# Seven tile pairs of a second dense product as exchanged 64-row halves, key and value weights in one load, and a new order

## The chip, the cores and the metric

The kernel runs on one core of a Trainium2 chip. The core has a matmul engine (PE, whose weight loads the profile shows apart as PEld), a vector engine (DVE), an activation engine (ACT), a general engine (POOL) and a queue engine (SP), which here issues nearly all transfers. The metric is the device time of one execution in microseconds; of the kernel before, three runs gave 151.16, 151.43 and 151.85, with the median 151.43. Lower is better.

## The reference

The sum of three terms over 2048 tokens of 448 values, all in bf16: the input, a linear attention over 16 heads of 28 whose features are softmaxes, and a dense product with Mish between its two weight matrices.

```python
xn = layernorm(x)                                    # x: 2048 x 448
q, k, v = split(xn @ wqkv)                           # 16 heads of 28
phi(y) = concat(softmax(y @ w_phi), softmax(-y @ w_phi))
kv = phi(k)^T v ;  z = sum over tokens of phi(k)
o = (phi(q) kv) / (phi(q) z + 1e-6)
h = xn @ w1 + b1                                     # 2048 x 1792
out = x + o @ wo + (h * tanh(softplus(h))) @ w2      # w2: 1792 x 448
```

## The kernel before

**Tiles.** The tokens are 16 tiles of 128, taken as 8 pairs u (tiles 2u and 2u+1). A row of 448 values is three and a half chunks of 128. The two tiles of a pair share the half chunk: the transposed input of a pair, `xnT[:, u]`, has seven chunks, of which the middle one holds the last 64 values of the one tile in partitions 0 to 63 and those of the other in partitions 64 to 127.

**Half-height passes.** All products over the 448 inputs are made with matmuls that use 64 of the array's 128 rows. Two of them, on different rows, are in the array together and write two different banks of PSUM, one for each tile of the pair. A unit of work on a pair has three parts: A (chunks 0 to 2; rows 0 to 63 work for the first tile and rows 64 to 127 for the second: 6 matmuls), B (the same with the rows exchanged, 6 matmuls) and H (the shared half chunk, 2 matmuls). `passes` lists them. A and H of a bank go on the same rows; B must not run into a bank while A or H does, so `pe_pass` makes each wait for the last part of the other kind on the same banks, and the order puts other work between.

**Steps.** The kernel is a list of named steps, `ORDER`, written out in the file. Each engine runs its instructions in the order in which the steps appear; `Program` derives the waits between engines from what each step reads and writes, and takes PSUM banks from a rotating pool, so the order also sets who waits for whose bank. The steps that matter here (u a pair, t a tile):

- `lx..`, `lkms`, `lvms`, `lkts`, `lps`, `lba`, `l1..`, `l2s`, `los`: loads of x, of the key and the value weights (rows 0 to 383), of the 64 last rows of both (the tails), of the feature weights (Wraw), of b1, of w1, w2 and wo. The last letter is the issuing engine, s for SP and a for ACT.
- `z12`: twelve matmuls on zeros. `b1`: the bias turned by PE. `pv`, `pk`, `pm`, `pw`, `pi`, `pp`, `zero`: constants, on POOL.
- `st`, `rs`, `xn`, `xt`: layer norm of a pair and its transposition. `rs2p` has POOL raise the variance to the power −0.5 (lines 470 and 473); the form with `a` uses a logarithm and an exponential on ACT (lines 476 and 478). `st2b` shares the statistics of a pair between DVE and ACT. `xt2b` and `xt3a` transpose on PE, `xt..m` by a transfer.
- `wtk`, `wmk`, `wmq`: the key and query weights are multiplied by `w_phi` on the chip (lines 556 and 580).
- `vuA`, `kuB`, `quH` and so on: the three products of a pair (line 423); the last part is followed by its evacuation, for k and q two exponentials on ACT.
- `kn`: normalisation of the key features (DVE, then POOL, line 630). `kvu`: the key-value product (line 649, into 32-column groups). `kvz`: its transposition.
- `fq.cA` and so on: first dense product, half q of the tokens, chunk c of 1792 (line 423), with Mish on ACT into `actT`.
- `ndt`: numerator and denominator (line 722, 16 narrow matmuls) and the DVE work on them; `ot`: the transposition of a pair of outputs.
- `woA`, `woB`, `woH`: product with wo (line 845); `gt`: second dense product of tile t (line 828), 14 matmuls over all 128 rows. Both add up in one bank per tile. When all four parts of a tile are in, `finish` adds x on DVE and the bank comes free. Tile 15 is last, and its last 64 columns are made apart (`last_columns`, lines 807 to 810).
- `sto`: stores.

**Queues.** SP, POOL and ACT each run in order. A transfer waits on its issuing engine for what it reads; what stands behind it in that engine's list waits too.

Of the kernel before, what the change touches and what calls it, by code (L numbers as in the profile page):

```python
# [12 lines left out]
D = 448  # L13
H = 16
DH = 28
F = 1792
P = 128
NT = S // P
NU = NT // 2
FC = F // P  # L20
G = 4
# [126 lines left out]
pv table lx2s lba zero pm st2b lx3s lkms lps st3b lkts z12 pi b1 rs2p pw rs3a xn2d bd lx1s wtk0b lvms lx4s xn3d xt2b  # L148
wtk1b wmk0b lqT2 xt3a v2Ha wmk1a v2Ba lqT0 st1 v3Ha lqT1 lqT3 rs1a v3Aa v2Aa st4 rs4p pk v3Ba k3H lx0s k3A qd xn1d
wmq0d wmq1a k2H k3B lx6s pp k2A st5 q3A xn4d k2B q3B rs5p q2A xt1m l1ts q3H k1A q2H xn5p xt4m st0 v1Ad k1H st6 xt5m e7  # L150
rs0p q2B st7 xn0d v1Bd k1B v1Hd rs7p rs6p k4A k4H q1B k4B xn6d q1H q1A v4Ad k5H xn7d v4Hd k5A v4Bd v5Ad kn1.0 xt0m k5B
v5Bd k0B xt6m v5Hd xt7m v0Ba kn2.1 kn2.0 k0H k0A e3 k6H k6A kn0.0 e2 v6Ba l1ms k6B v0Ha kn0.1 v0Aa v6Aa v6Ha k7H k7A
q4B e6 k7B v7Aa v7Ha kn7.0 q4H q4A q6A q6H v7Ba e9 q6B kn6.0 f0.2B kn5.1 f0.0A f1.2A f0.2A f0.0H f1.2H kn6.1 e5 f1.3B
f0.2H f0.0B e12 f1.2B f1.3A kn4.1 f0.3B kn5.0 f1.3H e13 f0.3H f0.1B e4 f0.3A f0.1H f0.1A q7H q0A kn3.1 q0H kn4.0 q5B
e8 q0B q7B kv5 kn7.1 e0 kv0 kv2 q7A q5A f0.13A q5H f0.13B kv7 kv4 e10 kv6 f0.13H f0.6H f0.6A kn3.0 f0.10A f0.6B kn1.1
f0.10B kv3 kv1 ep f0.10H f1.7H f1.7A e11 f1.9A kvz f1.7B f0.12B f1.5B f0.12A f1.5H f0.5H f1.9H f0.12H l2s f1.9B f1.5A
f0.5A f1.1A nd3 f1.1B f0.5B e15 f1.0A f1.1H f1.13B f1.0H f1.13H f1.0B nd2 los f1.13A ot1m f1.8B f0.9H f1.8A f1.8H nd0
f0.11B f0.9A f0.11A f0.11H f0.7A f0.7H f0.8B nd6 e14 f0.8H f0.9B f0.7B e1 f0.8A f1.12H f1.12A f1.10A nd7 f1.10B f1.4H
f1.10H f1.12B ot3m f1.4A nd1 f1.6B f1.4B f0.4H f1.6A ot0m f0.4A wo1H f1.6H f0.4B nd4 wo1A wo3A wo1B wo3H nd5 ot2m g1
g3 g2 f1.11A f1.11H nd11 wo0B f1.11B wo3B wo0A nd13 wo0H nd10 g6 ot5m g0 g7 g11 nd12 wo2A wo5A sto1 ot6m wo5H wo2B  # L160
nd15 nd9 g10 sto0 g5 nd14 ot7m wo2H wo5B nd8 g4 g9 g14 g13 g12 g8 sto3 ot4m wo4H wo4A wo6B wo7B sto2 wo6H wo6A sto5
wo4B sto4 wo7H wob wo7A g15 stt14 sto6 stt15
"""


def run_order(steps, order):
    for name in order:
# [811 lines left out]
```

## Time and profile before

| | us |
|---|---|
| median of three runs | 151.43 (151.16 to 151.85) |
| the profiled execution's own time | 150.73 |
| its span | 148.7 |
| PE busy in the span | 144.0 (97%) |
| DVE busy | 102.7 (69%) |
| ACT busy | 74.7 (50%) |
| POOL busy | 38.9 (26%) |

The profile is one execution, 2.0 us longer than its span. The page gives the busy time of each engine and the chain of work that ended last, followed back from the last instruction. Further views of the same execution give that chain in order of time, the instructions of one engine in a window, and the transfers with their time to landing. Matmuls overlap each other, so the length of one (some 0.35 us) is not what one costs: a stretch is divided by the matmuls in it. Line numbers are those of the kernel before; after the change, lines from 276 on lie 4 lower down.

### The profile page before, as it was taken

The numbers are of one execution on the slowest core, as the hardware profiler recorded it, in microseconds if no ns is written. First come the engines' busy times: TensorE is split into PE (matmuls) and PEld (weight loads), VectorE is DVE, ScalarE is ACT, GpSimd is POOL, SyncE is SP. The second block draws the span as 40 slices with busy tenths as digits, with TensorE's granted clock in tenths as the row PEclk, the third lists the DMA queues.
The fourth block names the chain that finished last, engine by engine and source line by source line (L and its number), as shares of the span: only waits on it lengthen the run. The fifth ranks groups of instructions, "written<-read, shape, count | busy, mean of one in ns | idle before, by whom it ended". The sixth has DMA issues, their size and how long they took to land.

```text
span 148.7 us, 3864 instructions
## 1 busy us (share of the span) xinstructions
PE 144.0 (97%) x1669; PEld 74.2 (50%) x1669; DVE 102.7 (69%) x229; ACT 74.7 (50%) x91; POOL 38.9 (26%) x53
## 2 busy tenths in 40 slices
PE   6899999999999999999999999999999999999992
PEld 2365555555444555444444445545555555555561
DVE  0699898996999930407787989529983999930072
ACT  4997999779999999567747661002000000000000
POOL 4424465179999992000000000000000000000000
PEclk9999999999999999999999999999999999999999
DMA  4997997799699069499956053210013130551005
GB/s 131 245 278 216 119 185 149 126 170 344 103 188 196 14 52 132 85 239 295 195 98 125 4 62 62 43 23 0 7 37 86 35 93 0 123 127 58 4 10 175
DMA packets 39964, 17.23 MB, mean 116 GB/s; under 512 B 33932, under 2 KB 39180, under 8 KB 39948
## 3 DMA queue, kind: packets, MB, share of 16 engines
q1 hardware_dynamic: 39776, 16.89, 54.4%
q8 instruction: 13, 0.21, 0.6%
q10 hardware_dynamic: 172, 0.10, 0.2%
q14 instruction: 3, 0.02, 0.0%
HBM read 7.02 MB, written 1.84 MB: 60 GB/s over the span
## 4 chain that ended last, share of the span: by engine, by line
PE 92%; DMA 3%; DVE 2%; SPq 1%; issue 0%
PE PS L423 50%; PE PS L828 29%; PE PS L845 7%; DMA Wkv<-in_A_wqkv_dram 3%; PE PS L722 3%; PE PS L649 2%; PE PS L580 1%; DVE xn L497 1%; SPq L270 1%; PE PS L556 0%; PE PS L505 0%; DVE x_all L793 0%; DVE Eq L512 0%; DVE x_all L814 0%
## 5 line engine op out<-in xcount | busy, mean ns | idle before, releaser
L423 PE MATMUL PS<-xnT,W 64*128 64x512 bf16 x392 | 44.8, 377 | 0.0
L828 PE MATMUL PS<-W,actT 128*128 128x448 bf16 (+1 forms) x224 | 42.9, 351 | 0.0
L699 ACT ACTIVATE actT<-PS,b1T 128x1024 bf16<-128x1024 f32 x28 | 29.8, 1112 | 22.1 <-PE PS L423 22.1
L828 PEld LDWEIGHTS PS<-W,actT 128*128 128x128 bf16 x224 | 21.5, 98 | 19.8 <-issue 0.3
L423 PEld LDWEIGHTS PS<-xnT,W 64*128 64x128 bf16 x392 | 17.9, 94 | 21.9 <-PE PS L423 1.9
L630 POOL TENSOR_TENSOR actT<-actT,rSk 128x896 bf16<-128x896 bf16 x16 | 26.6, 1699 | 5.1 <-DVE rSk L628 5.1
L793 DVE TENSOR_TENSOR x_all<-PS,x_all 128x448 bf16<-128x448 f32 (+1 forms) x16 | 9.2, 613 | 15.2 <-PE PS L845 10.5
L626 DVE TENSOR_REDUCE Sk<-actT 128x32 f32<-128x896 bf16 x16 | 16.6, 1037 | 1.1 <-ACT actT L618 1.1
L618 ACT ACTIVATE actT<-PS 128x896 bf16<-128x896 f32 x16 | 13.7, 920 | 1.8 <-PE PS L423 1.7
L423 PE MATMUL PS<-Wpk,xnT 64*128 64x448 bf16 x112 | 13.2, 349 | 0.0
L423 PE MATMUL PS<-Wkv,xnT 64*128 64x448 bf16 x112 | 12.9, 349 | 0.0
L423 PE MATMUL PS<-Wpq,xnT 64*128 64x448 bf16 x112 | 12.6, 349 | 0.0
L738 DVE COPY Sq<-PS 128x16 f32<-128x16 f32 x32 | 4.0, 167 | 12.0 <-PE PS L722 12.0
L462 DVE BATCH_NORM_STATS2 stats<-x_all 128x6 f32<-128x448 bf16 x14 | 8.4, 601 | 3.4 <-DMA x_all<-in_A_x_dram 3.4
L746 DVE TENSOR_TENSOR v_all<-v_all 128x464 f32<-128x464 f32 x16 | 10.3, 641 | 0.6
L742 DVE TENSOR_TENSOR v_all<-PS,Sq 128x464 f32<-128x464 f32 x16 | 10.3, 641 | 0.5
L749 DVE TENSOR_TENSOR xn<-v_all,rden 128x448 bf16<-128x448 f32 x16 | 10.0, 625 | 0.6
L744 DVE TENSOR_TENSOR v_all<-PS,Sq 128x464 f32<-128x464 f32 x16 | 10.1, 629 | 0.0
L680 ACT ACTIVATE actT<-PS 128x896 bf16<-128x896 f32 x10 | 8.6, 930 | 0.1
L423 PEld LDWEIGHTS PS<-Wpq,xnT 64*128 64x128 bf16 x112 | 5.4, 94 | 5.0 <-ACT actT L680 0.2
L423 PEld LDWEIGHTS PS<-Wkv,xnT 64*128 64x128 bf16 x112 | 5.4, 94 | 5.1 <-ACT actT L618 0.2
L423 PEld LDWEIGHTS PS<-Wpk,xnT 64*128 64x128 bf16 x112 | 5.3, 94 | 5.1 <-issue 0.2
(83 smaller groups left out, 118.8 us busy)
## 6 DMA issues: line engine op xcount, KB each, us to landing
W<-in_B_w_dram SPq DMA_DIRECT2D x1, 1568.0 KB, 7.9
out_dram<-x_all SPq DMA_DIRECT2D x7, 224.0 KB, 2.2
W<-in_B_w_dram SPq DMA_DIRECT2D x1, 1344.0 KB, 7.0
x_all<-in_A_x_dram SPq DMA_DIRECT2D x4, 224.0 KB, 3.1
x_all<-in_A_x_dram SPq DMA_DIRECT2D x2, 448.0 KB, 4.9
Wkv<-in_A_wqkv_dram SPq DMA_DIRECT2D x2, 336.0 KB, 4.8
Wo<-in_A_wo_dram SPq DMA_DIRECT2D x2, 336.0 KB, 6.3
W<-in_B_w_dram SPq DMA_DIRECT2D x2, 224.0 KB, 4.1
```

What stands on the lines that cost most here:

```text
L423: ins = e.matmul(o, lhs(c, k), rhs(c, k), start=first and n == at[par][0], stop=last and n == at[par][-1])
L618: op("ACT", lambda e, s=s: e.activation(E_of(u)[:, s, :, :], two(b, D), ACT.Exp, scale=1.0 if s == 0 else -1.0), r=[pb(b), pb(b + 1)], w=[ ...
L626: op("DVE", lambda e: e.tensor_reduce(Sk[u][:, s, :], Eh(), AX.X, ALU.add), r=[("E", u, s)], w=[("Sk", u, s)], tag=f"Sk{u}.{s}")
L630: op("POOL", lambda e: e.tensor_tensor(Eh(), Eh(), ap_on(rSk[u][:, s, 0:1], [[1, 2 * H], [0, DH]]), ALU.mult), r=[("E", u, s), ("rSk", u, ...
L699: op("ACT", lambda e: e.activation(actT[:, fc, q * 1024:(q + 1) * 1024], bank(b, 2), ACT.Mish, bias=b1T[:, fc:fc + 1]), r=[("b1T",), pb(b) ...
L742: op("DVE", lambda e: e.tensor_tensor(tv(t1[i]), num(0), sx(1), ALU.mult), r=[pb(b), pb(b + 1), ("Sq", i, 1)], w=[("t1", i)], tag=f"ta{t}")
L744: op("DVE", lambda e: e.tensor_tensor(tv(t2), num(1), sx(0), ALU.mult), r=[pb(b), pb(b + 1), ("Sq", i, 0)], w=[("t2",)], tag=f"tb{t}")
L746: op("DVE", lambda e: e.tensor_tensor(t1[i], t1[i], t2, ALU.add), r=[("t1", i), ("t2",)], w=[("t1", i)], tag=f"tc{t}")
L749: op("DVE", lambda e: e.tensor_tensor(o_sb[(t // 2) % 2][:, t % 2, :].rearrange("p (h d) -> p h d", d=DH), t1[i][:, :, 0:DH], ap_on(rden[i ...
L793: op("DVE", lambda e: e.tensor_tensor(x_all[:, t, 0:n], bank(b)[:, 0:n], x_all[:, t, 0:n], ALU.add), r=[pb(b), ("x", t)], w=[("out", t)], ...
L828: ins = e.matmul(bank(b)[:, 0:width(t)], actT[:, fc, tok(t)], W2[:, fc, 0:width(t)], start=first and fc == 0, stop=last and fc == FC - 1)
L845: ins = e.matmul(bank(b)[:, 0:w], oT_of(u)[lo:hi, cc * P:(cc + 1) * P], Wo[lo:hi, cc, 0:w], start=first and n == at[par][0], stop=last and ...
```

## The change

It has four parts.

1. **Second dense product.** For pairs 0 to 6 the two steps `g2u` and `g2u+1` give way to `GuA` and `GuB`: 28 half-height matmuls each, over the 14 chunks, rows 0 to 63 for the one tile and rows 64 to 127 for the other, and exchanged in B. The helper `out_pair` is shared with the wo parts. A tile of these pairs then has five parts (two of G, three of wo), and both tiles of a pair come to an end with the same part. Pair 7 keeps g14 and g15.
2. **Weights.** One load brings key and value weights (384 rows, of both matrices) where two loads brought 336 KB each.
3. **First pair's norm power** on ACT (`rs2a`; the first pair worked on is pair 2) where it was on POOL; the statistics of the second, pair 3, are all on DVE (`st3`), where they were shared with ACT. b1's load is issued behind the first statistics on ACT.
4. **A new order** of all steps. At the start value products stand ahead of the feature products; at the end the G parts lie between nd steps and wo parts; the q, k, v and f parts between them are in another order as well.

PE at the start, before (L364 the matmuls on zeros, L693 the bias, L556 the transposes of the key weights, L505 those of xn, L580 the feature products, L423 the products of a pair):

```order
L364 MATMUL PS<-zeros 128x512 x12
L693 MATMUL PS<-ident,b_rows 128x14
L556 MATMUL PS<-ident,Wkv 112x128 x8
L505 MATMUL PS<-ident,xn 128x128 x7
L556 MATMUL PS<-ident,Wkv 112x128 x8
L580 MATMUL PS<-Wbd,Eq 128x112 x8
L505 MATMUL PS<-ident,xn 128x128 x7
L423 MATMUL PS<-Wkv,xnT 128x448 x2
L580 MATMUL PS<-Wbd,Eq 128x112 x8
L423 MATMUL PS<-Wkv,xnT 128x448 x26
L423 MATMUL PS<-Wpk,xnT 128x448 x8
```

and in the change, where the same lines have 4 added:

```order
L368 MATMUL PS<-zeros 128x512 x12
L697 MATMUL PS<-ident,b_rows 128x14
L509 MATMUL PS<-ident,xn 128x128 x7
L560 MATMUL PS<-ident,Wkv 112x128 x8
L509 MATMUL PS<-ident,xn 128x128 x7
L560 MATMUL PS<-ident,Wkv 112x128 x8
L427 MATMUL PS<-Wkv,xnT 128x448 x14
L584 MATMUL PS<-Wbd,Eq 128x112 x16
L427 MATMUL PS<-Wkv,xnT 128x448 x14
L427 MATMUL PS<-Wpk,xnT 128x448 x6
```

The transposes of xn now stand ahead of those of the key weights, the two L584 groups are together, and fourteen value matmuls stand ahead of them.

PE towards the end, before (L828 the second dense product, L845 the wo parts, L722 the nd matmuls):

```order
L722 MATMUL PS<-KVZ,EqT 128x60 x16
L828 MATMUL PS<-W,actT 128x448 x56
L722 MATMUL PS<-KVZ,EqT 128x60 x16
L845 MATMUL PS<-Wo,Wkv 128x448 x6
L845 MATMUL PS<-Wo,WqT 128x448 x8
L845 MATMUL PS<-Wo,Wkv 128x448 x6
L722 MATMUL PS<-KVZ,EqT 128x60 x32
L828 MATMUL PS<-W,actT 128x448 x28
L722 MATMUL PS<-KVZ,EqT 128x60 x16
L845 MATMUL PS<-Wo,Wkv 128x448 x2
L845 MATMUL PS<-Wo,WqT 128x448 x6
L722 MATMUL PS<-KVZ,EqT 128x60 x16
```

and in the change, where L848 holds both the wo parts (those from Wo) and the half-height parts of the second product (those from W, actT):

```order
L848 MATMUL PS<-Wo,Wkv 128x448 x2
L848 MATMUL PS<-W,actT 128x448 x28
L726 MATMUL PS<-KVZ,EqT 128x60 x16
L848 MATMUL PS<-Wo,Wkv 128x448 x8
L848 MATMUL PS<-W,actT 128x448 x28
L726 MATMUL PS<-KVZ,EqT 128x60 x16
L848 MATMUL PS<-Wo,Wkv 128x448 x12
L848 MATMUL PS<-W,actT 128x448 x28
L726 MATMUL PS<-KVZ,EqT 128x60 x16
L848 MATMUL PS<-W,actT 128x448 x28
L726 MATMUL PS<-KVZ,EqT 128x60 x16
L848 MATMUL PS<-Wo,Wkv 128x448 x6
```

Long runs of the full-height form are gone from here; what stands in their place are runs of 28 half-height matmuls between nd and wo parts.

SP at the start, before (L270 x, L273 the main weights, L278 their tails, L282 the transposed query weights, L293 the feature weights):

```order
L270 DMA x_all<-in_A_x_dram 128x896 x2
L273 DMA Wkv<-in_A_wqkv_dram 128x3x448
L293 DMA Wraw<-in_A_w_phi_dram 112x4x28
L278 DMA Wkv<-in_A_wqkv_dram 64x896 x2
L270 DMA x_all<-in_A_x_dram 128x896
L273 DMA Wkv<-in_A_wqkv_dram 128x3x448
L270 DMA x_all<-in_A_x_dram 128x1792
L282 DMA_TRANSPOSE WqT<-in_A_wqkv_dram 128x448 x4
L270 DMA x_all<-in_A_x_dram 128x896
L270 DMA x_all<-in_A_x_dram 128x1792
```

and in the change (L277 is the joint load):

```order
L270 DMA x_all<-in_A_x_dram 128x896 x2
L277 DMA Wkv<-in_A_wqkv_dram 128x3x896
L297 DMA Wraw<-in_A_w_phi_dram 112x4x28
L282 DMA Wkv<-in_A_wqkv_dram 64x896 x2
L270 DMA x_all<-in_A_x_dram 128x896
L270 DMA x_all<-in_A_x_dram 128x1792
L286 DMA_TRANSPOSE WqT<-in_A_wqkv_dram 128x448 x4
L282 DMA W<-in_B_w_dram 64x1792 x2
L521 DMA_TRANSPOSE xnT<-xn 128x7x128
L270 DMA x_all<-in_A_x_dram 128x896
L270 DMA x_all<-in_A_x_dram 128x1792
```

The second weight load is gone, the first is twice as wide, and the tails of w1 have moved ahead of the last two loads of x.

The diff, with the table of steps cut to its first line:

```diff
-pv table lx2s lba zero pm st2b lx3s lkms lps st3b lkts z12 pi b1 rs2p pw rs3a xn2d bd lx1s wtk0b lvms lx4s xn3d xt2b
+table lx2s st2b lba zero pi lx3s lkvs lps pv lkts z12 rs2a st3 pk xn2d rs3a xn3d lx1s b1 xt2b wtk0b lx4s xt3a st1
...
+    def load_kv(eng):
+        dma(eng, lambda e: e.dma_start(Wkv[:, 0:3, :], A_wqkv[0:384, D:3 * D].rearrange("(c p) f -> p c f", p=P)),
+            w=[("Wk", 0), ("Wv", 0)], tag="ldKV")
...
     def parts_of(t):
-        return 3 if f"wo{t // 2}F" in STEPS else 4
+        return (2 if f"wo{t // 2}F" in STEPS else 3) + (2 if f"G{t // 2}A" in STEPS else 1)
...
-    def wo(u, part):
+    def out_pair(u, part, todo, works, r, tag):
         places = [out_part(2 * u + par) for par in range(2)]
-        todo = passes(part)
 
         def f(e):
             at = {par: [n for n, x in enumerate(todo) if x[1] == par] for par in range(2)}
-            for n, (c, par, (lo, hi)) in enumerate(todo):
+            for n, (c, par, k) in enumerate(todo):
                 b, first, last = places[par]
-                cc = xchunk(c, par)
                 w = width(2 * u + par)
-                ins = e.matmul(bank(b)[:, 0:w], oT_of(u)[lo:hi, cc * P:(cc + 1) * P], Wo[lo:hi, cc, 0:w],
-                               start=first and n == at[par][0], stop=last and n == at[par][-1])
+                lhs, rhs = works(c, par, k, w)
+                ins = e.matmul(bank(b)[:, 0:w], lhs, rhs, start=first and n == at[par][0], stop=last and n == at[par][-1])
             return ins
-        pe_pass(f, [("oT", u)] + [("Wo", n) for n in range(4)], places[0][0], part, f"wo{u}{part}")
+        pe_pass(f, r, places[0][0], part, tag)
         for par, (b, first, last) in enumerate(places):
             if last:
                 finish(2 * u + par)
+
+    def wo(u, part):
+        def works(c, par, k, w):
+            cc = xchunk(c, par)
+            return oT_of(u)[k[0]:k[1], cc * P:(cc + 1) * P], Wo[k[0]:k[1], cc, 0:w]
+        out_pair(u, part, passes(part), works, [("oT", u)] + [("Wo", n) for n in range(4)], f"wo{u}{part}")
+
+    def ffn2_pair(u, part):
+        x = int(part == "B")
+
+        def works(fc, par, k, w):
+            return actT[k[0]:k[1], fc, tok(2 * u + par)], W2[k[0]:k[1], fc, 0:w]
+        out_pair(u, part, [(fc, r ^ x, HALF[r]) for fc in range(FC) for r in range(2)], works,
+                 [("W2",)] + [("act", fc, u // 4) for fc in range(FC)], f"G{u}{part}")
```

More of the change, by code (lines that the diff above doesn't have):

```diff
@@ L158 @@
[L158 to L162, printed above, removed]
+table lx2s st2b lba zero pi lx3s lkvs lps pv lkts z12 rs2a st3 pk xn2d rs3a xn3d lx1s b1 xt2b wtk0b lx4s xt3a st1
@@ L884, in _kernel @@
             add(f"wo{u}{part}", wo, u, part)
+        for part in "AB":
+            add(f"G{u}{part}", ffn2_pair, u, part)
         for s in range(2):
@@ L911, in _kernel @@
             add(f"l{n}m{c}", load_main, eng, "W" + n, t, A_wqkv[:, (i + 1) * D:(i + 2) * D])
+        add(f"lkv{c}", load_kv, eng)
         add(f"lkt{c}", load_tail, eng, "Wkv", Wkv, A_wqkv[:, D:3 * D])
```

23 lines of the change are left out of this document (14 added, 9 removed).

## The prediction

> **What bounds the kernel now.** I read the page's totals first, then the chain that ended last, in order of time, then the first twelve microseconds engine by engine, then the transfers.
>
> The page, its totals and the shares of its chain:
>
> ```profile
> span 148.7 us, 3864 instructions
> PE 144.0 (97%) x1669; PEld 74.2 (50%) x1669; DVE 102.7 (69%) x229; ACT 74.7 (50%) x91; POOL 38.9 (26%) x53
> PE 92%; DMA 3%; DVE 2%; SPq 1%; issue 0%
> ```
>
> PE carries 92% of the chain, and nothing beside the first load and the last store holds it up. So the change is worth what it does to PE's own stream, plus what it does to the moment when the dense stream begins. The chain in order of time (start, length, what):
>
> ```profile
> 1.72 4.95 DMA Wkv<-in_A_wqkv_dram
> ...
> 9.92 0.50 PE PS L580 x8
> 10.42 3.32 PE PS L423 x34
> ...
> 50.89 0.88 PE PS L649 x96
> ...
> 58.55 0.64 PE PS L649 x64
> ...
> 67.30 3.93 PE PS L423 x36
> ...
> 88.60 1.89 PE PS L845 x20
> 90.49 0.22 PE PS L722 x16
> 90.71 8.05 PE PS L828 x42
> 98.76 0.97 PE PS L423 x8
> ...
> 113.64 0.33 PE PS L722 x16
> ...
> 116.30 5.40 PE PS L828 x28
> 121.70 0.33 PE PS L722 x16
> ...
> 123.01 16.00 PE PS L828 x84
> ```
>
> **Term 1: the matmuls of the second product.** L828 is the full-height form (128 rows, 448 columns). The three pieces give two unknowns: (16.00 − 5.40) / 56 = 0.189 us for one matmul, and 5.40 − 28 × 0.1893 = 0.10 us left over at the start of a run (8.05 − 42 × 0.1893 = 0.10 as well). L845 is the 64-row form of the same width: 1.89 / 20 = 0.0945 each, 0.189 for a pair that does one full-height matmul's work. The 392 new half-height matmuls (7 pairs of tiles × 2 parts × 28) therefore cost the same as the 196 they replace: zero, within 0.1 us. The 64-row weights that each needs load beside the running matmuls, as they do under L845.
>
> **Term 2: switches between the two forms.** A run of L828 pays 0.10 at its start. At its end the next piece pays: 16 matmuls of L722 take 0.22 after half-height work (90.49) but 0.33 after L828 (113.64, 121.70), so 0.11; the eight L423 at 98.76 take 0.97, where 8 × 3.93 / 36 = 0.87. One switch is 0.10. Before has four runs of L828 inside half-height work (g1 g3 g2; g6 g0 g7 g11; g10 g5; g4 to g8), 8 switches, and one into g15. After has one switch, into g14 g15. Eight fewer: −0.8 us. The key-value product L649 is also a different form: (0.88 − 0.64) / 32 = 0.0075 each, 0.64 − 64 × 0.0075 = 0.16 to enter; leaving it I put at the 0.10 above. Three runs of it become two: −0.25. Together −1.05 us. Switches at the start stay five and five, by the order.
>
> On these the Trainium skill, "TensorEngine Tiling (Array Packing)", section "Key Properties", says that changing the tiling mode drains the array. It gives no time; the rows' 0.10 is used.
>
> **Term 3: the start.** What stands on the engines (PE, ACT, POOL, DVE, SP) up to 9 us:
>
> ```profile
> 1.39 4.80 PE L364 MATMUL PS<-zeros 128*128 128x512 bf16 x12 [1.39 <-POOL mask L327]
> 6.72 0.65 PE L556 MATMUL PS<-ident,Wkv 128*112 128x128 bf16 x8 [0.43 <-DMA Wkv<-in_A_wqkv_dram]
> 7.38 0.56 PE L505 MATMUL PS<-ident,xn 128*128 128x128 bf16 x7
> 7.85 0.65 PE L556 MATMUL PS<-ident,Wkv 128*112 128x128 bf16 x8
> 4.37 0.67 ACT L458 ACTIVATE junk<-x_all,rmean 128x448 bf16<-128x448 bf16 x1
> 6.75 0.29 ACT L476 ACTIVATE lnv<-mv,eps_col 128x2 f32<-128x2 f32 x1
> 7.07 0.20 ACT L478 ACTIVATE rstd<-lnv 128x2 f32<-128x2 f32 x1
> 0.80 0.53 POOL L339 MEMSET v_all<- 128x256 uint32 x1 [0.29 <-POOLq L964]
> 5.52 0.71 POOL L473 TENSOR_TENSOR rstd<-lnv,mhalf 128x2 f32<-128x2 f32 x1
> 4.19 0.59 DVE L462 BATCH_NORM_STATS2 stats<-x_all 128x6 f32<-128x448 bf16 x1
> 4.82 0.18 DVE L464 BATCH_NORM_AGGREGATE mv<-stats 128x2 f32<-128x6 f32 x1
> 6.42 0.90 DVE L497 TENSOR_SCALAR xn<-x_all,mv,rstd 128x448 bf16<-128x448 bf16 x3
> 0.84 0.63 ACTq L297 DMA_DIRECT2D b_rows<-in_B_b_dram  x1
> ```
>
> Transfers: KB each, us to landing.
>
> ```profile
> W<-in_B_w_dram SPq DMA_DIRECT2D x1, 1344.0 KB, 7.0
> x_all<-in_A_x_dram SPq DMA_DIRECT2D x4, 224.0 KB, 3.1
> x_all<-in_A_x_dram SPq DMA_DIRECT2D x2, 448.0 KB, 4.9
> Wkv<-in_A_wqkv_dram SPq DMA_DIRECT2D x2, 336.0 KB, 4.8
> W<-in_B_w_dram SPq DMA_DIRECT2D x2, 224.0 KB, 4.1
> Wkv<-in_A_wqkv_dram SPq DMA_DIRECT2D x2, 112.0 KB, 4.6
> ```
>
> Norm power on ACT: the squares end at 5.04; logarithm and exponent take 0.29 + 0.20 and two gaps of some 0.05, so 5.6, where POOL's power ended at 6.23. DVE meanwhile takes the second pair's other statistics (0.59 + 0.18 from 4.9), free at 5.7. Its three scalings (0.90) end at 6.65 and the first transposes of xn can start at 6.7, not 7.38. The bias load, issued on ACT behind the squares (4.4 to 5.0 by its 0.63), feeds a small transpose that stands ahead on PE. No landing is listed for it; I bound it by an issue's end plus 1.0 (the first x load, of 224 KB, lands 3.1 after its issue began) and by 4.1, the 224 KB row under traffic, and take the first: 3.5 KB. The end near 4.1 would put it at 8.5 and cost 1.7.
>
> The joint load is 672 KB where the keys alone were 336, and PE needs the keys. Below: the 112 and 336 KB rows differ by 0.2 in 224 KB, +0.3 for 336 KB more. Above: the x rows, 1.8 us in 224 KB, +2.7. Between: the W1 rows, 2.9 us over 1120 KB, +0.87. The number of source rows stays 384, only their width doubles, and it is ahead of the same small loads; I take +0.6, nearest to the W1 slope. By the Trainium skill, "DMA: Bandwidth & Descriptors", section "Anatomy of one DMA", bytes move at 436 GB/s, an estimate of 0.79; the sum would then be −0.75.
>
> So the keys land at 6.67 + 0.6 = 7.27, and the tails behind them, which released 7.85, at 8.45. PE: xn transposes 6.7 to 7.2, keys' 7.3 to 7.9, second xn transposes to 8.4, keys' second half 8.45 to 9.05. Before's dense stream ran from 10.36 (the L423 behind the L580 of 9.92) with one H part (0.19) and two L580 groups (0.50 with a switch, so 0.40 each) already done. After owes these, and three switches: 9.05 + 0.19 + 0.80 + 0.30 = 10.34. Term 3 is zero, from −0.3 to +2.1 by the ends of the load's price. What hides the value half of the load: its own first use is later still (the H part behind 9.05). Behind the keys on SP wait the small Wraw load, the tails and x; the separate value load is no longer issued there, so the WqT transposes move up by one issue, and x's first pair with them; the W1 tails now stand ahead of the last two x loads, whose statistics stand well behind on DVE.
>
> **Term 4: ACT.** The tightest place that I find is between the last exponentials and Mish (ACT):
>
> ```profile
> 50.85 1.73 ACT L680 ACTIVATE Eq<-PS 128x896 bf16<-128x896 f32 x2
> 52.48 3.35 ACT L680 ACTIVATE actT<-PS 128x896 bf16<-128x896 f32 x4
> 55.84 1.28 ACT L699 ACT_TABLE_LOAD   x1
> 57.14 2.12 ACT L699 ACTIVATE actT<-PS,b1T 128x1024 bf16<-128x1024 f32 x2
> ```
>
> After: from q5's last part to f1.0's first, ACT does six exponentials (4.98), a table load (1.3) and three Mish (3.1): 9.4. PE has q and f parts and eight kv steps between: two q parts of 6 and one of 2 (14 × 0.0945), eight f parts of 6 and four of 2 (56 × 0.109), 7.4 together, and 256 × 0.0075 + 2 × 0.26 = 2.4 for kv: 9.9. It holds, by half a us. Elsewhere the chain of before shows no wait for an evacuation, and I take the new order to keep its distances about as well; I add +0.1 for such waits, from 0 to +1. The tail is the same: g15, eighteen narrow matmuls, two additions, two stores.
>
> **Sum.** −1.05 + 0 + 0.1 = −0.95 against the profiled execution's own 150.73 (span 148.7 and 2.0 around it), which lies 0.7 under the median 151.43. On the median: 150.5.
>
> **Rivals.**
> - *The joint load holds the start.* If it lands 1.6 us later than the keys did instead of 0.6, the gain is gone; at the x rows' +2.7 the time is 151.43 − 0.95 + 2.1 = 152.6. For it: PE's first wait is this load (0.43 at 6.72), and all later loads queue behind it. Against: 112 and 336 KB land alike. Chance 0.13.
> - *The gain is lost in waits, no change: 151.4.* The two parts of a pair may not follow each other: the second waits for the end of the first, since other rows then write the bank. Between G0A and G0B stand only 16 narrow matmuls and one H part (0.22 + 0.22), and 64-row banks are held longer, as half of an output is done early. With ACT's margin this could cost 1 us. Against: L845 and L423 do the same now and the chain shows no wait of theirs. Chance 0.18.
> - *The clock comes later.* The twelve warm-up matmuls took 0.40 us each for 512 columns, when 448 take 0.189 later: half rate up to some 5.5 us. After starts them some 0.4 earlier (the zeros are POOL's first and no longer stand behind its memset of 0.53) and leaves PE idle for longer, from about 5.8 to 6.7. If full rate came only at 9, the 2.1 us of transposes would double: 150.5 + 2.1 = 152.6. The Trainium skill, "TensorE: Matmul & The Clock Gate", section "What's actually happening", has the clock rise after a busy window of about 3.4 us that is free-running, so the moment may fall badly; the one trace cannot show it. Chance 0.07.
> - *A better start*: keys at +0.3 and the bias at once, everything 0.3 earlier: 150.2 and, with no wait on ACT, 150.1; below 149.6 only if a switch is dearer than 0.10. Chance of that 0.02.
>
> **How the numbers follow.** The forecast (149.6 to 150.9) has 0.60, the rivals 0.18, 0.13, 0.07 and 0.02. A measurement of this kernel tells about 0.5% (0.75 us) from no change, so faster begins under 150.7. The forecast's upper edge lies over that: of its 0.60, 0.52 is faster. Faster 0.52 + 0.02 = 0.54; same 0.08 + 0.18 = 0.26; slower 0.13 + 0.07 = 0.20. The range 149.6 to 152.2 takes in the forecast, the case of no change and the nearer half of both slow rivals.
>
> **What would show it.** The chain after: one L828-like run of 28 at the end; pairs of the second product at 0.189; 16 narrow matmuls at 0.22 throughout. Keys' transposes near 7.3 and their second half near 8.45; POOL's first power gone. Wrong if PE waits for the joint load beyond 8, if a wait of PE on Mish or on its own earlier part appears, or if the pairs take over 0.195.

## The result and the profile after

The changed kernel takes 154.86 us (median of six, 153.75 to 155.37) where the kernel before takes 151.36 beside it (150.80 to 151.85): 1.0227 times as long, interval 1.0201 to 1.0253. It was forecast 150.5 us, 0.6% faster; it is 3.5 us slower. The profiled execution took 154.04, 2.0 more than its span, and before's 150.73, so the two traces differ by 3.3. Medians here and below are of all executions of a kernel; where the granted clock parts them into groups, the groups are given.

The page of the changed kernel, its totals, its granted clock (a digit for each fortieth of the span, in tenths of the full clock, 9 for 90% or more) and the shares of its chain:

```profile
span 152.0 us, 4252 instructions
PE 144.7 (95%) x1865; PEld 77.9 (51%) x1865; DVE 102.8 (68%) x231; ACT 73.9 (49%) x88; POOL 37.9 (25%) x51
PEclk9987999999999999999999999999999999999999
PE 91%; DMA 5%; ACT 1%; DVE 0%; issue 0%
```

PE's work is 0.7 us longer (144.7 against 144.0), the span 3.3. So most of the loss is time in which PE had nothing to do. The chain in order of time (start, length, what) says where:

```profile
4.64 5.38 DMA b_rows<-in_B_b_dram
10.02 0.05 issue
10.07 0.19 PE PS L697
10.26 0.86 PE PS L509 x7
11.12 0.85 PE PS L560 x8
11.97 0.75 PE PS L509 x7
12.72 0.79 PE PS L560 x8
13.50 1.43 PE PS L427 x14
...
57.12 1.72 PE PS L653 x160
...
62.88 1.01 PE PS L653 x96
...
89.36 2.65 PE PS L848 x28
92.00 0.22 PE PS L726 x16
...
143.94 5.07 PE PS L832 x28
149.00 0.02 issue
```

The bias load, 3.5 KB issued on ACT behind the squares, is 5.38 us on the way, and PE's first real work (L697, the transposition of the bias) stands behind it. Only then come the transposes of xn and of the key weights (L509, L560). They end at 13.50. By the prediction's account of what was still owed there (one H part, two groups of feature products, three switches: 1.29 us), this is the point 14.79 of a stream that before reached at 10.36: 4.43 us late. From there to PE's last matmul it is 134.2 us (149.00 − 14.79), where before it was 135.0 (145.40 − 10.36). The two rows of before for this, the first from the list of PE's instructions, the second from the chain:

```profile
10.36 2.63 PE L423 MATMUL PS<-Wkv,xnT 64*128 64x448 bf16 x26
142.98 2.42 PE PS L828 x14
```

The new stream is 0.8 us shorter, and another 0.3 is saved behind the last matmul. The start costs 4.4, four times what these two save.

Two things make the start late. One is the wait: the zeros end at 6.25 (3.19 after the start of the first window below), and the transposition of the bias begins at 10.07. The other is the clock. The windows of 3.41 us around it (busy time and, in brackets, instructions of each engine; then granted clock, share of the DMA engines, GB/s):

```profile
core 0: us, PE busy (x) PEld busy (x) DVE busy (x) ACT busy (x) POOL busy (x), PEclk, DMA share, GB/s
3.06:6.47 3.41, 3.19 (x8) 0.88 (x6) 2.67 (x8) 2.54 (x9) 0.63 (x2) 1.00 0.89 247
6.47:9.89 3.42, 0.00 (x0) 0.00 (x0) 1.21 (x5) 0.09 (x1) 0.64 (x2) 1.00 1.08 256
9.89:13.30 3.41, 3.23 (x31) 3.21 (x31) 1.86 (x6) 1.63 (x3) 0.43 (x1) 0.50 1.38 198
13.30:16.71 3.41, 3.41 (x43) 1.97 (x43) 2.99 (x9) 2.48 (x6) 0.00 (x0) 1.00 0.36 95
```

PE has nothing to do from 6.47 to 9.89, and for exactly the next 3.41 us the clock is granted at half. In that stretch fall the transposes: in the list of PE's instructions their groups take 0.93 to 1.06 us, where groups of the same kinds took 0.56 and 0.65 before. Half the clock for 3.41 us takes 1.1% off the mean of a span, so the mean clock of an execution tells how many such stretches it had: 1.0 none, 0.989 one, 0.978 two. Two of the six executions of the changed kernel had one (153.75, 154.04) and four had two (154.85 to 155.37). The kernel before had none: its mean clock was 0.997 or more in all executions beside the experiments. No trace holds a second stretch, so where it lies is not shown.

The joint load, issued at 1.73, landed 7.1 us later, at about 8.8:

```profile
Wkv<-in_A_wqkv_dram SPq DMA_DIRECT2D x1, 672.0 KB, 7.1
```

Here that is hidden behind the bias. Between 18.7 us and PE's last matmul nothing stands in the chain's rows but PE, so no wait on ACT, on Mish or between the two parts of a pair became visible.

### The profile page after: what moved, and what is told of

It is laid out like the page before. It is cut to its first block, busy times and chain, and to the rows that moved or that the text cites. A ratio compares the mean times of both kernels' runs of the same rounds, so it can differ in the third digit from the quotient of the medians.

```text
span 152.0 us, 4252 instructions
## 1 busy us (share of the span) xinstructions
PE 144.7 (95%) x1865; PEld 77.9 (51%) x1865; DVE 102.8 (68%) x231; ACT 73.9 (49%) x88; POOL 37.9 (25%) x51
## 4 chain that ended last, share of the span: by engine, by line
PE 91%; DMA 5%; ACT 1%; DVE 0%; issue 0%
PE PS L427 49%; PE PS L848 31%; DMA b_rows<-in_B_b_dram 4%; PE PS L832 3%; PE PS L726 2%; DMA x_all<-in_A_x_dram 2%; PE PS L653 2%; PE PS L584 1%; PE PS L560 1%; PE PS L509 1%; ACT junk L457 0%; DVE x_all L797 0%; ACT rmean L460 0%; DVE x_all L818 0%; PE PS L697 0%
## 5 line engine op out<-in xcount | busy, mean ns | idle before, releaser
L848 PE MATMUL PS<-W,actT 64*128 64x448 bf16 x392 | 39.4, 349 | 0.0
L848 PEld LDWEIGHTS PS<-W,actT 64*128 64x128 bf16 x392 | 21.1, 94 | 15.2
L466 DVE BATCH_NORM_STATS2 stats<-x_all 128x6 f32<-128x448 bf16 x15 | 9.1, 607 | 3.7 <-DMA x_all<-in_A_x_dram 3.7
```

The lines of the kernel that those rows point to most:

```text
L466: op("DVE", lambda e, t=t: e.bn_stats(stats[:, t, :], x_all[:, t, :]), r=[("x", t)], w=[("st", t)], tag=f"bn{t}")
L848: ins = e.matmul(bank(b)[:, 0:w], lhs, rhs, start=first and n == at[par][0], stop=last and n == at[par][-1])
```

## The experiments

The theory formed from this trace: the whole loss lies in two loads at the start, the bias load's place on ACT and the joint load, together with the clock that falls when PE waits for them; all else of the change does about what was forecast. The rivals: the new order loses time somewhere that the chain does not show; or the halves cost more than full-height matmuls. Medians of the kernel before beside these runs lay between 151.19 and 151.36; differences to it below use 151.2.

### The bias load back ahead of the statistics

```diff
-table lx2s st2b lba zero pi lx3s lkvs lps pv lkts z12 rs2a st3 pk xn2d rs3a xn3d lx1s b1 xt2b wtk0b lx4s xt3a st1
+table lx2s lba st2b zero pi lx3s lkvs lps pv lkts z12 rs2a st3 pk xn2d rs3a xn3d lx1s b1 xt2b wtk0b lx4s xt3a st1
```

> The changed kernel with only the load of the bias moved back ahead of ACT's first statistics, where the kernel before has it. Theory B (the late bias load holds PE from 6.3 to 10.1 and lets the clock fall, and is the whole loss at the start): PE starts near 7.3, time 150.3 to 150.7. Theory B+J (behind it the joint load, which landed at 8.87, is the next bound): the key transposes wait for it to 8.9, dense stream some 1.5 us later than before's, less 0.8 from PE's stream: 151.6 to 152.4, up to 1.1 more if the clock still falls. Theory J alone (the joint load is the cause, the bias is not): no change, 154.5 to 155.

Measured: 152.34 (ten executions, 149.85 to 153.19), 2.5 less than the changed kernel. Eight of the ten had one stretch of half clock (152.21 to 153.19); the two without one took 149.85 and 151.09. PE at the start, and the two windows of the clock:

```profile
6.05 0.18 PE L697 MATMUL PS<-ident,b_rows 14*128 14x14 bf16 x1
6.75 0.56 PE L509 MATMUL PS<-ident,xn 128*128 128x128 bf16 x7 [0.52 <-DVE xn L501]
8.80 0.71 PE L560 MATMUL PS<-ident,Wkv 128*112 128x128 bf16 x8 [1.49 <-DMA Wkv<-in_A_wqkv_dram]
```

```profile
5.86:9.27 3.41, 1.40 (x17) 0.95 (x17) 2.04 (x8) 0.97 (x3) 0.00 (x0) 1.00 1.11 262
9.27:12.68 3.41, 3.41 (x29) 2.38 (x28) 2.36 (x7) 2.55 (x5) 1.08 (x2) 0.50 1.43 245
```

xn is ready at 6.75, as the prediction had it (6.7). But now the joint load comes to light: PE waits 1.49 for the key weights, until 8.80 and not 7.27. And after a window in which PE was busy for 1.40 of its 3.41 us the clock fell.

### The same bias load late, in the kernel before

```diff
-pv table lx2s lba zero pm st2b lx3s lkms lps st3b lkts z12 pi b1 rs2p pw rs3a xn2d bd lx1s wtk0b lvms lx4s xn3d xt2b
+pv table lx2s zero pm st2b lba lx3s lkms lps st3b lkts z12 pi b1 rs2p pw rs3a xn2d bd lx1s wtk0b lvms lx4s xn3d xt2b
```

> The kernel before with only the load of the bias moved behind ACT's first squares. Theory B: the bias lands near 9 to 10, PE waits for it, and the time rises by 3 to 4 us to 154.4 to 155.4, with a fall of the clock. Theory J alone: the bias is not the cause, below 152.

Measured: 154.47 (153.67 to 155.10), 1.0212 of before (1.0165 to 1.0260). One name moved by three places in the table costs the kernel before nearly as much as the whole change cost. PE's wait for it:

```profile
9.21 0.16 PE L693 MATMUL PS<-ident,b_rows 14*128 14x14 bf16 x1 [2.52 <-DMA b_rows<-in_B_b_dram]
```

and the load's own time under way, from the chain:

```profile
4.42 4.66 DMA b_rows<-in_B_b_dram
```

### Early bias and two loads of the weights

```diff
-table lx2s st2b lba zero pi lx3s lkvs lps pv lkts z12 rs2a st3 pk xn2d rs3a xn3d lx1s b1 xt2b wtk0b lx4s xt3a st1
+table lx2s lba st2b zero pi lx3s lkms lps pv lkts z12 rs2a st3 pk xn2d rs3a xn3d lx1s b1 xt2b wtk0b lvms lx4s xt3a st1
```

> The changed kernel with the early bias load and with key and value weights again in two loads, the values behind x's first pair. If the prediction's terms for PE's stream hold (0.8 us gained) and the start is like before's or 0.3 better: 150.2 to 150.8. If the joint load did not matter: the same as with the early bias alone.

Measured: 150.25 (150.18 to 151.25), 0.9935 of before (0.9914 to 0.9955). With both loads put back the rest of the change gives 0.95 us, as much as the prediction's sum; how much of that is luck stands under "The sum" below. No execution had a stretch of half clock. PE at the start:

```profile
6.18 0.19 PE L697 MATMUL PS<-ident,b_rows 14*128 14x14 bf16 x1
6.72 0.58 PE L509 MATMUL PS<-ident,xn 128*128 128x128 bf16 x7 [0.35 <-DVE xn L501]
7.19 0.65 PE L560 MATMUL PS<-ident,Wkv 128*112 128x128 bf16 x8
8.30 0.62 PE L560 MATMUL PS<-ident,Wkv 128*112 128x128 bf16 x8
9.64 1.50 PE L427 MATMUL PS<-Wkv,xnT 64*128 64x448 bf16 x14 [0.72 <-DMA Wkv<-in_A_wqkv_dram]
```

The transposes run almost without a gap from 6.72; what PE waits for now is the value half of the weights, 0.72 us until 9.64, since the new order puts value products first.

### The joint load alone, in the kernel before

```diff
-pv table lx2s lba zero pm st2b lx3s lkms lps st3b lkts z12 pi b1 rs2p pw rs3a xn2d bd lx1s wtk0b lvms lx4s xn3d xt2b
+pv table lx2s lba zero pm st2b lx3s lkvs lps st3b lkts z12 pi b1 rs2p pw rs3a xn2d bd lx1s wtk0b lx4s xn3d xt2b
```

> The kernel before with only the two weight loads made one. Theory B+J: keys land near 8.9 where they landed at 6.7, PE's first real work is 1.5 to 2.2 us later, 152.9 to 153.6. If the joint load does not matter (its landing at 8.87 would then be due to the later order of other loads): 151.2 to 151.9.

Measured: 153.63 (153.63 to 154.12), 1.0168 of before (1.0145 to 1.0191): +2.4. Every execution had one stretch of half clock. The key weights come at 8.33, where they came at 6.72; busy for 1.71 us of a window, PE loses the clock in the next:

```profile
8.33 0.65 PE L560 MATMUL PS<-ident,Wkv 128*112 128x128 bf16 x8 [1.55 <-DMA Wkv<-in_A_wqkv_dram]
```

```profile
6.51:9.93 3.42, 1.71 (x24) 1.36 (x24) 1.88 (x6) 1.61 (x6) 1.47 (x3) 1.00 1.35 265
9.93:13.34 3.41, 3.41 (x32) 2.54 (x32) 3.34 (x11) 2.22 (x5) 0.06 (x1) 0.50 1.04 203
```

So each of the two loads costs over 2 us by itself, in either kernel, the stretch of half clock that it brings included.

### Two loads, the bias load late

Early or late bias, one load or two: this run is the fourth corner of that square.

```diff
-table lx2s st2b lba zero pi lx3s lkvs lps pv lkts z12 rs2a st3 pk xn2d rs3a xn3d lx1s b1 xt2b wtk0b lx4s xt3a st1
+table lx2s st2b lba zero pi lx3s lkms lps pv lkts z12 rs2a st3 pk xn2d rs3a xn3d lx1s b1 xt2b wtk0b lvms lx4s xt3a st1
```

> The changed kernel with two weight loads in place of the joint one, and the bias load left behind the first statistics on ACT. It completes a square: late bias with joint load 154.86, early bias with joint load 152.34, early bias with two loads 150.25. Theory (PE stands first for the bias load, and the loads in front of it set its landing; the joint load alone would hold the keys' transposes, which come later): the bias lands near 9.2 as in the kernel before with its bias load moved, PE begins 3 us later than in the best version, 0.45 of it is taken back where that one waits at v1A, and the clock falls for one window (1.2): 153.5 to 154.3. Rival (the joint load is the larger cost and the bias only lands late because of it): 151.0 to 152.0.

Measured: 152.91 (twelve executions, 150.98 to 154.69). Neither expectation's range holds it: the wait and the fall of the clock are where the theory has them, its price was 0.6 to 1.4 too high. The bias landed earlier than taken, at 8.57, with 336 KB less in front of it than in the changed kernel. The executions order themselves by the mean clock: one at 1.0 took 150.98; seven at 0.989 took 152.19 to 153.23; four at 0.978 took 153.89 to 154.69. By the medians of these groups a stretch of half clock costs some 1.7 us here. The chain of the profiled one (0.989):

```profile
4.51 4.01 DMA b_rows<-in_B_b_dram
...
8.57 0.19 PE PS L697
```

The square, medians in us:

| | two loads | joint load | difference |
|---|---|---|---|
| bias early | 150.25 | 152.34 | +2.1 |
| bias late | 152.91 | 154.86 | +2.0 |
| difference | +2.7 | +2.5 | |

The two add up within 0.2 us: each costs about as much beside the other as alone. But these medians mix executions with and without the half clock. Where the clock held, the early bias with the joint load took 149.85 and 151.09, and the late bias with two loads 150.98, at most 0.8 over 150.25. So in these three executions, which are few, most of the price of one load alone is the fall of the clock behind its wait, and not the wait.

### The changed kernel with PE kept busy until the bias lands

How much of the loss is the clock? Thirty matmuls on zeros instead of twelve, and nothing else changed.

```diff
-table lx2s st2b lba zero pi lx3s lkvs lps pv lkts z12 rs2a st3 pk xn2d rs3a xn3d lx1s b1 xt2b wtk0b lx4s xt3a st1
+table lx2s st2b lba zero pi lx3s lkvs lps pv lkts z30 rs2a st3 pk xn2d rs3a xn3d lx1s b1 xt2b wtk0b lx4s xt3a st1
```

> The changed kernel as it is (late bias load, joint load), with 30 matmuls on zeros in place of 12, so that PE is busy until the bias lands near 10. It separates the clock from the wait. Theory (a partly idle stretch lets the clock fall for 3.4 us, and this is a part of the loss): the mean clock is 1.0, the transposes of xn take 0.56 and not 0.85 to 0.93, and the time is 154.86 - 1.5 to 2.1 = 152.8 to 153.4; what is left over 150.5 is the wait itself. Rival (the clock's fall costs little, since the transposes wait for evacuations anyway): 154.4 to 154.9.

Measured: 153.70 (153.29 to 154.71), 1.2 less than the changed kernel, just outside the theory's range and well away from the rival's. The clock is 1.0 in the profiled execution (0.999 or more in all four), and the transposes of xn take 0.56 us again:

```profile
0.95 8.47 PE L368 MATMUL PS<-zeros 128*128 128x512 bf16 x30 [0.95 <-POOL mhalf L323]
10.02 0.18 PE L697 MATMUL PS<-ident,b_rows 14*128 14x14 bf16 x1 [0.60 <-DMA b_rows<-in_B_b_dram]
10.13 0.56 PE L509 MATMUL PS<-ident,xn 128*128 128x128 bf16 x7
...
11.91 1.56 PE L427 MATMUL PS<-Wkv,xnT 64*128 64x448 bf16 x14
```

The value products begin at 11.91 instead of 13.50, 1.6 earlier; PE's last matmul ends at 147.5 instead of 149.0 by the chain. (What follows it, the last store above all, took 0.9 longer in this one execution, so the spans differ by 0.6.) Work that does nothing makes the kernel faster. Of the 3.45 us that remain over 150.25, the traces show 2.3 as the plain wait for the two loads: the value products begin at 11.91, and at 9.64 in the kernel with both loads put back. The longer tail of the profiled execution is another 0.9; whether the other executions have it is not shown.

### Early bias, joint load, twenty zeros

The same idea on the kernel with the early bias, whose wait is shorter.

```diff
-table lx2s lba st2b zero pi lx3s lkvs lps pv lkts z12 rs2a st3 pk xn2d rs3a xn3d lx1s b1 xt2b wtk0b lx4s xt3a st1
+table lx2s lba st2b zero pi lx3s lkvs lps pv lkts z20 rs2a st3 pk xn2d rs3a xn3d lx1s b1 xt2b wtk0b lx4s xt3a st1
```

> The changed kernel with the early bias load, the joint load kept, and twenty matmuls on zeros at the start instead of twelve, so that PE is busy until the keys land near 8.8. Theory C (the wait costs little by itself; what costs is that PE's idle time lets the clock fall to half for one window of 3.4 us): no window at half rate, 150.0 to 151.1 in every execution. Rival W (the wait for the joint load is the cost): 152.2 to 153.2, as with the early bias alone.

Measured: 152.54 (ten executions, 150.45 to 154.04), no gain over 152.34, though nine of the ten kept the clock at 1.0. Only two (150.45, 150.72) lie in the theory's range. In the profiled execution (152.53) the time came back in a second wait, 45 us later, PE's rows first and ACT's behind them:

```profile
55.84 1.70 PE L653 MATMUL PS<-actT,v_all 128*30 128x56 bf16 x160 [1.61 <-ACT actT L684]
```

```profile
52.77 1.28 ACT L684 ACT_TABLE_LOAD   x1 [1.69 <-issue]
```

The key-value products wait for exponentials, and ACT had stood from 51.08 to 52.77. The chain has in front of it a transposing transfer that SP issued at 47.70. It took 5.0 us to land, so until 52.70, where the three issued before it took 3.3 to 3.4; why it took longer is open. This is the one execution that has a trace; that the slower ones of the other nine have the same cause is not shown.

### The bias load late, its transposition late too

Is it the load, or that PE stands first for it? Two weight loads, the bias load as late as in the change, and its transposition moved from PE's first place to some 9 us later.

```diff
-table lx2s st2b lba zero pi lx3s lkvs lps pv lkts z12 rs2a st3 pk xn2d rs3a xn3d lx1s b1 xt2b wtk0b lx4s xt3a st1
+table lx2s st2b lba zero pi lx3s lkms lps pv lkts z12 rs2a st3 pk xn2d rs3a xn3d lx1s xt2b wtk0b lvms lx4s xt3a st1
...
-k2A rs4p st5 k3H xt1m rs5p xn4d pp k3A xn5p q3B k3B v1Ad lx0s v1Hd st0 rs0p q1B lx6s xt4m q3H q3A xt5m v1Bd st7 q2H
+k2A rs4p st5 k3H xt1m rs5p xn4d pp k3A xn5p b1 q3B k3B v1Ad lx0s v1Hd st0 rs0p q1B lx6s xt4m q3H q3A xt5m v1Bd st7 q2H
```

> The changed kernel with two weight loads; the bias load stays late, behind ACT's first squares, but the bias's transpose on PE stands some 9 us further back, among the first k and q parts. Theory B (the late load hurts only because PE's first step waits for it): as with the early load and two weight loads, 150.1 to 150.5. Rival (the late load disturbs the other transfers or ACT): over 151.

Measured: 151.04 (150.47 to 152.10), 0.9991 of before (0.9966 to 1.0017), clock 1.0. The theory's range ends at 150.5, and the rival's begins where this median lies. A late load that nobody stands for costs 0.8 us over the early one, not 2.7: most of the price hangs on the place of the load's first user in PE's queue. Where the 0.8 comes from is not shown.

### The first pair's norm power back on POOL

The prediction had this part bring xn forward from 7.38 to 6.7, within a start that came to zero; its own worth stayed open. From the kernel with early bias and two loads:

```diff
-table lx2s lba st2b zero pi lx3s lkms lps pv lkts z12 rs2a st3 pk xn2d rs3a xn3d lx1s b1 xt2b wtk0b lvms lx4s xt3a st1
+table lx2s lba st2b zero pi lx3s lkms lps pv lkts z12 rs2p st3 pk xn2d rs3a xn3d lx1s b1 xt2b wtk0b lvms lx4s xt3a st1
```

> The changed kernel with early bias load and two weight loads, and the first pair's norm power on POOL again. Theory: xn is ready 0.6 us later (near 7.4), but the first value part waits for the value weights to 9.6 in either case, so 150.2 to 150.5. Rival (the power on ACT is worth its 0.6 us): 150.7 to 150.9.

Measured: 152.22 (twelve executions, 151.04 to 152.93), 2.0 over 150.25, where both theories expected under 0.7. Four executions kept the clock (151.04 to 151.53); eight had one stretch of half clock (152.16 to 152.93). The profiled one kept it:

```profile
7.53 0.56 PE L509 MATMUL PS<-ident,xn 128*128 128x128 bf16 x7 [1.15 <-DVE xn L501]
```

xn is ready at 7.53, not 6.72. So the power on ACT is worth 0.9 us where the clock holds, and in most executions it also keeps the clock from falling.

### The pairs undone

From the kernel with early bias and two loads, each G part replaced by one full-height step at its place: 14 runs of the full-height form instead of one, 26 switches more.

```diff
-wo0A f1.8H f1.8A nd11 wo0H G2B nd10 wo0B wo3H ot2m G3A nd13 wo2B wo3B ot5m G2A nd12 G1B ot6m nd15 wo1A G3B nd14 G1A
+wo0A f1.8H f1.8A nd11 wo0H g5 nd10 wo0B wo3H ot2m g6 nd13 wo2B wo3B ot5m g4 nd12 g3 ot6m nd15 wo1A g7 nd14 g2
...
```

> The changed kernel with early bias load and two weight loads, and the fourteen half-height parts of the second product put back to full-height steps at the same places of the order (even tile for A, odd tile for B). Same work, 36 switches between the forms instead of 10. Theory: 26 x 0.092 = 2.4 us over the same kernel with halves (150.25), 152.4 to 152.9. Rival (a switch is hidden, or halves are slower by themselves): 150.0 to 150.5.

Measured: 153.13 (153.02 to 153.67), 2.9 more than 150.25 and 0.2 above the theory's range. From its chain:

```profile
86.14 2.76 PE PS L832 x14
88.89 0.33 PE PS L726 x16
```

Against 2.65 and 0.22 in the changed kernel's chain: 0.10 on entering the full-height form, 0.11 on leaving it. Twenty-six of these are 2.7; the other 0.2 stays open. The matmuls themselves cost the same either way: 2.76 less the 0.10 on entering is 2.66 for 14 of them, and 28 halves took 2.65.

### The pairs alone, in the kernel before

The kernel before with G parts at the places of its g steps, and g14 next to g15.

```diff
-nd15 nd9 g10 sto0 g5 nd14 ot7m wo2H wo5B nd8 g4 g9 g14 g13 g12 g8 sto3 ot4m wo4H wo4A wo6B wo7B sto2 wo6H wo6A sto5
-wo4B sto4 wo7H wob wo7A g15 stt14 sto6 stt15
+nd15 nd9 G5A sto0 G2B nd14 ot7m wo2H wo5B nd8 G4A G5B G6A G4B G6B sto3 ot4m wo4H wo4A wo6B wo7B sto2 wo6H wo6A sto5
+wo4B sto4 wo7H wob wo7A g14 g15 stt14 sto6 stt15
```

> The kernel before with the first part of the change alone: the steps g0 to g13 of its order give way to the pair parts at the same places, pairs 1 and 3 first, and g14 goes next to g15; its start, its loads, and its order of everything else stay. Theory (a pair costs what a full-height matmul costs, and a switch between the forms 0.092 to 0.10): eight switches fewer, 151.2 - 0.74 to 0.80 = 150.4 to 150.5. Rival (the two parts of a pair, which may not run into one another, and the banks held longer, cost what the switches bring): 151.0 to 151.6, with a wait of PE among the parts of the second product.

Measured: 153.55 (153.15 to 155.26), 1.0180 of before (1.0136 to 1.0224): 2.3 slower, where the theory said 0.8 faster. The rival's waits are there, but dearer than its no change. At one place PE waits long:

```profile
125.70 4.51 PE L848 MATMUL PS<-W,actT 64*128 64x448 bf16 x28 [2.13 <-DVE v_all L748]
```

A pair opens two banks at once and holds them to its last part; behind nd8 the next two banks are still being read by DVE for nd outputs. G4A waits 2.13 us for them. In this order g4 needed one bank. Two more waits of PE on DVE near there are shorter (0.3 and 0.2 by the list of waits). The window up to 126.54 then held only 1.28 us of PE work, and behind it the profiled execution lost its clock here too, over 120 us into the kernel:

```profile
126.54:129.95 3.41, 3.41 (x22) 1.42 (x20) 3.31 (x9) 0.00 (x0) 0.00 (x0) 0.50 0.44 95
```

So at these places the pairs lose more than the switches bring; in the change's order, which spreads them, its trace shows no such wait. Which part stands at which g's place was chosen for this run; another choice might wait less.

### A run of small matmuls parted

In the profile of the kernel with early bias and two loads (its execution took 150.93, its median is 150.25) PE stands for 0.65 us inside the run of five key-value products, released by nothing that the profile shows:

```profile
55.12 0.67 PE L653 MATMUL PS<-actT,v_all 128*30 128x56 bf16 x62 [0.65 <-issue]
```

```diff
-q7A e4 q5H los q7H q5A q0A q5B q0H f0.6B q7B q0B kv6 kv7 kv0 e11 kv2 kv5 f0.6A f0.13B f0.6H f0.13A f0.5B e10 f0.13H
+q7A e4 q5H los q7H q5A q0A q5B q0H f0.6B q7B q0B kv6 kv7 kv0 e11 f0.6A kv2 kv5 f0.13B f0.6H f0.13A f0.5B e10 f0.13H
```

> The kernel with the early bias load and two weight loads (150.25), with its run of five key-value products (160 small matmuls, in which PE stood 0.65 us on 'issue' in the profile) parted by the six matmuls of f0.6A: 96, then 64. Theory (the stall comes from the length of the run of small matmuls): the stall of 0.65 goes, two switches between forms come (0.16 to 0.26): 149.75 to 149.85. Rival (the stall comes with the load of PE's next instructions and stays wherever it falls): 150.25 + 0.2 = 150.45, and PE's wait on 'issue' of 0.5 or more is still there.

Measured: 150.20 (thirteen executions, 150.08 to 151.57), 0.9933 of before (0.9909 to 0.9956): no different from 150.25. In the profiled execution, at 151.57 the slowest of the thirteen, the wait is still there, between two f matmuls now:

```profile
55.85 0.60 PE L427 MATMUL PS<-xnT,W 64*128 64x512 bf16 x4 [1.13 <-issue]
```

The theory falls: the run's length is not the cause. The wait is about as long as that execution lies over the others (1.13, and 151.57 − 150.20 is 1.4; 0.65, and 150.93 − 150.25 is 0.7), so it seems to come in some executions and not in most. In both traces a packet of 16 KB on the profile's queue of instructions begins shortly before (at 53.46 and at 52.51). The changed kernel's trace has one at 54.93 and no such wait, so that this is the cause is not shown.

## Why the prediction was wrong

**Term 1, the halves at the price of full-height matmuls: right.** A part of 28 takes 2.65 us in the changed kernel's chain, 0.189 for a pair of halves, as forecast.

**Term 2, the switches: right for the second product, not for the key-value products.** A switch costs 0.10 to 0.11 (above). But two runs of key-value products in place of three did not bring their 0.25: in the chains the two take 1.72 and 1.01, together 2.73, and the three took 0.88, 0.88 and 0.64, together 2.40. Why the run of 160 is dearer is open. The stream behind the start became 0.8 shorter, not 1.05, with 0.3 more at the tail. The Trainium skill, "TensorEngine Tiling (Array Packing)", section "Key Properties", says that a change of tiling mode drains the array and gives no time for it; the rows of the second product put 0.10 to 0.11 us to it.

**Term 3, the start: this step failed.** "Term 3 is zero" was 4.4 us off in the trace. Two of its lines were priced too low, and what their waits do to the clock was left out of it.

- *The bias load.* The prediction bounded it by an issue's end plus 1.0 and by 4.1, "and take the first: 3.5 KB". It took 5.38, more than the upper bound. Its size does not explain that, what was already under way does: in the kernel before, which issues it at 0.84, its 28 packets are through by 2.8 us; in the changed kernel, which issues it at 4.64, all 28 lie between 7.8 and 9.6, and in the window up to 9.89 the DMA engines move 256 GB/s. Issued late beside two weight loads it took less, 4.01 us in the changed kernel (issued at 4.51, released PE at 8.57) and 4.66 in the kernel before (issued at 4.42). At 256 GB/s the 336 KB that differ are 1.3 us, an estimate; the times under way differ by 1.4 and by 0.7. The price named for the far end, 1.7, was low as well: measured 2.5 to 2.7 in the changed kernel and 3.2 in the kernel before, the fall of the clock included. The Trainium skill, "DMA: Bandwidth & Descriptors", section "Issuing engines are not separate DMA queues", says that transfers from different issuing engines run on the same 16 engines and interleave; the waits here agree that a queue of its own gave this load no way past the others.
- *The joint load.* "I take +0.6, nearest to the W1 slope"; the key weights came 1.6 us later in the kernel before (8.33 against 6.72), and in the changed kernel with its bias early at 8.80 instead of the 7.27 forecast. In the windows of the wait the engines moved 256 to 265 GB/s, which makes 336 KB worth 1.3 us, an estimate: between the two bounds, at twice the value chosen, and still under the 1.6 measured. The prediction's estimate of 0.79 by the Trainium skill, "DMA: Bandwidth & Descriptors", section "Anatomy of one DMA", was low too; the section gives its 436 GB/s for transfers that the general engine issues, and SP issues this one. "Wrong if PE waits for the joint load beyond 8" named the right sign. The rival on this load named 1.6 us late as the point where the gain is gone and 152.6 as the time at its far end, 2.7 late. The kernel with the early bias shows 152.34, but the load is 2.1 late there (8.80 against 6.72) and the clock's fall makes up the rest; that the two times are close is luck.
- *The clock.* The rival had a late first grant in mind, at 9 us. The first record of the full clock in the changed kernel's trace is at 6.47; what came was a fall after a window that PE spent waiting, for exactly one window of 3.41 us. The mechanism in the rival was wrong and its direction right. One stretch more costs 1.2 us in the changed kernel and 1.9 with the early bias and the joint load, by the medians of the groups; that the rival's price of 2.1 lies near is luck. It was treated as a rival by itself, when it is what a wait at the start can bring with it.

**"Term 3 is zero" also leaned on the power on ACT.** That step was right: with the power on ACT and twelve zeros, the transposes of xn began at 6.72 to 6.79 wherever the bias did not stand ahead, against 6.7 forecast. Undone, it costs 0.9 where the clock held, and 2.0 in the median.

**Term 4, ACT's waits: right for the changed kernel.** Its chain has no wait of this kind, and the place named as the tightest is one: in the kernel with twenty zeros the last exponentials before the key-value products held PE for 1.61 us, behind a transfer that landed late.

**The rival of waits between the parts of a pair** did not happen in this order, and did in the order of before (2.13 us for banks).

**The sum.** The two loads and the clock add 4.6 us (154.86 − 150.25) that Term 3 had at zero. By the traces, the value products begin at 9.64 with both loads put back and, in the changed kernel, at 13.44: 2.3 of this is the wait (until 11.91 with thirty zeros) and 1.5 the stretch of half clock. The second stretch, which four executions of six had, is about the rest.

With the two loads put back the forecast of 150.5 meets 150.25, and this is in part luck. In that kernel's trace the value products' 9.64 and the 1.29 still owed make 10.93, so its start is 0.6 later than before's 10.36 and not even. The stream gives back 0.8, without its stall of 0.65, and the tail 0.3: together 0.5 faster than before's profiled execution, and not 0.95. The medians show 0.95 because before's profiled execution, at 150.73, lies 0.5 under its median of 151.2.

## What to carry to other kernels

Price a small load by what is already in the queues when it is issued, and ask first which engine's first instruction stands behind it: 3.5 KB issued 4 us later cost 2.5 us and more. At the start, where the DMA engines are busy throughout, count the bytes ahead of the first needed tile at the rate of that window in the profile (256 to 265 GB/s here), not at a slope between two other loads. And add to an early wait of PE the stretch of half clock that may follow it, 1.2 to 1.9 us here. Matmuls on zeros that cover the wait gained 1.2 us in one kernel here and nothing in another.

## What the runs showed of the hardware

**The clock fell for one window after a window in which PE had little work.** The windows are 3.41 us long and begin at another moment in each execution (the first record of the full clock is at 4.55, 5.53, 6.47 and 6.99 us in four of the traces). In profiled executions the clock fell after windows with 0.00, 0.75, 0.93, 1.28, 1.40 and 1.71 us of PE work, and held after windows with 1.96, 2.64, 2.81 and 2.98; one window of 1.59 held as well, so by PE's busy time the border is somewhere near half and not sharp. The same kernel shows both cases (152.19 and 151.13 with the power on POOL); that the phase of the windows decides between them fits the rows and is not shown. The Trainium skill, "TensorE: Matmul & The Clock Gate", section "What's actually happening", has the clock at half after one or more idle windows of about 3.4 us that run free; the length and the free phase agree, but a window need not be idle: 1.71 us of work in it did not keep the clock.

**Waits move.** Keeping the clock by zeros saved 1.2 us in the changed kernel and nothing with the early bias; in the one trace of the latter a transfer from SP that took 5.0 us and not 3.3 held ACT, and through it PE, 45 us later.

**A wait of PE that nothing in the profile releases**, 0.37 to 1.21 us near 55 us, in five of the traces of the changed kernel's variants. Its cause is open.
